# Retention and two feed-forward layers on one core: layer-1 work among the head pairs in units of two f, rectifier on ScalarE

## The chip, the cores and the metric

The kernel runs on one core of one Trainium2 chip. The metric is the device time of one execution in microseconds (us); the number that counts is the median over timed executions. A core has five engines with instruction streams of their own: TensorE (PE in the profile, with its weight loads as PEld), VectorE (DVE), ScalarE (ACT), GpSimd (POOL), and SyncE (SP), which issues the DMAs. They meet only at semaphores. Each engine takes its own instructions in the order of the program.

## What is computed

```
scores = scale * q @ k.T                 # 4 batches, 8 heads, 576 positions, head size 64
ret    = scores * gamma ** rel           # causal: 0 where the key lies after the query
x      = ret @ v                         # -> 2304 tokens x 512
h1 = x @ w1_in    (512 x 2048);  x = max(0.01 * h1, h1) @ w1_out   (2048 x 512)
h2 = x @ w2_in    (512 x 2048);  out = (h2 - tanh(h2)) @ w2_out    (2048 x 512)
```

The weights come in as 64-bit floats. Everything else is 32 bits wide.

## The kernel before

**Weights.** Each layer has 16 blocks f of 128 hidden columns, and each f two weight pieces, one in and one out, of 128 x 512. A piece is loaded (512 KB), turned from 64 into 32 bits by five operations (`narrow_ops`: begin, clamp, shift, top, low; during the retention begin is on ScalarE and the other four on VectorE, later all five are on VectorE), and split into a rounded high part (ScalarE, L161) and the rest (GpSimd, L162). Activations are split the same way, so a product of two 128-blocks takes three matmuls: high times high, high times low, low times high.

**Layers.** The f are handled in groups of four. A step is one f of one token block: `h_mm` (12 matmuls into h), the nonlinearity (`act_a`, `chain`), and two steps later `o_mm` (12 matmuls, which add up over the four f of a group), then `evac`. Token blocks are 512 wide, and one of 256 in each group. While a group runs, `plan` spreads the narrowing of the next group's eight pieces over its steps.

**Retention.** It runs ahead of the layers over 16 head pairs (4 batches with 4 pairs each). In pair i the program emits `scores(i)` and `scores_tail(i)` (TensorE), `mask(i)` (VectorE, reads both), then the outputs of the pair before: `outputs_far(i-1)`, `outputs_near(i-1)`, then `states_mm(i)`, `finish(i-1)` (xh by ScalarE, xl by VectorE) and `states(i)` (VectorE). A head has four full chunks of 128 positions and a tail of 64. The tail's scores `t_sc` and the tail's output `o_tail` are two ranges of one PSUM tile, `x_a`.

**What lies among the pairs.** Group 0 of layer 1 is begun during the retention: three token blocks of 256 (`EARLY`), 12 steps in all, one f at a time, from pair 5 on (`pace`). Its eight weight pieces are prepared by `fill`, which emits the list `ops` (54 entries, about seven for each piece) between the parts of the pairs; the table `at_pair` says how many entries are done by the end of each pair:

```
            at_pair = [7, 10, 14, 17, 24, 28, 38, 46, 53]
            pace = [0] * (NP + 1) + [1] * 10 + [2]
```

The order of the instructions on each engine is the order in which the program emits them; no scheduler moves them.

Of the kernel before, what the change touches and what calls it, by code (L numbers as in the profile page):

```python
# [18 lines left out]
P = 128  # L19
CH = 128  # L20
# [13 lines left out]
def retention_moe_moe(  # L34
# [152 lines left out]
    def act_a(s):  # L187
# [22 lines left out]
    def chain(s):  # L210
        m, g, t0, n, f = steps[s]
        h = hp.pop(s)[:, :n]
        if m == 0:
            v = tmp.pop(s)[:, :n]
# [8 lines left out]
        gt = pools["g"].tile([P, 2, pools["w"]], F32R, tag="g", name="g")  # L223
        nc.scalar.activation(out=gt[:, 0, :n], in_=v, func=AF.Copy)  # L224
        nc.gpsimd.tensor_tensor(  # L225
# [79 lines left out]
    def retention():  # L305
        with ExitStack() as ac:
            ak = ac.enter_context(tc.tile_pool(name="ak", bufs=1))
            ap_ = ac.enter_context(tc.tile_pool(name="ap", bufs=3))
            pools["t"] = ac.enter_context(tc.tile_pool(name="t0", bufs=2))
            pools["g"] = ac.enter_context(tc.tile_pool(name="g0", bufs=3))  # L310
            cw_pool[0] = ac.enter_context(tc.tile_pool(name="c0", bufs=2))
            ps_s = ac.enter_context(tc.tile_pool(name="ps_s", bufs=1, space=PSUM))
            pools["a"] = ac.enter_context(tc.tile_pool(name="ps_a0", bufs=2, space=PSUM))
            pools["w"] = QW
# [5 lines left out]
            pools["h"] = lambda s: x_b[:, :QW]  # L320

# [5 lines left out]
            bds = [ak.tile([P, 2, TAIL], F32, name=f"bd{i}") for i in range(2)]  # L327
            qk, kv, pts, cs_ = {}, {}, {}, {}
            order = [(b, p) for b in range(B) for p in range(NP)]
# [56 lines left out]
            def scores_tail(i):  # L386
                nc.tensor.matmul(
                    out=t_sc, lhsT=qk[i][:, 0, S - CH:], rhs=bds[i % 2], start=True, stop=True
                )

            def mask(i, sc):
# [10 lines left out]
                for h in range(2):  # L402
                    nc.vector.scalar_tensor_tensor(
                        out=pt[:, h, MAIN:], in0=t_sc[:, h, :], scalar=back[h],
                        in1=cm_sb[:, 0, CH:], op0=ALU.mult, op1=ALU.mult,
                    )
                pts[i] = pt

            def states_mm(i):
                t = kv[i]  # L410
                c_ = ps_s.tile([P, NFULL, 64], F32, tag="c", name="c")
                for c in range(NFULL):
                    for h in range(2):
# [4 lines left out]
                        )  # L418
                cs_[i] = c_

            def states(i):
                b, p = order[i]
                c_, st = cs_.pop(i), sts[i % 2]
                for h in range(2):
# [27 lines left out]

            def outputs_near(i, o_):
                pt, t = pts.pop(i), kv.pop(i)
                for c in range(NCH):
                    dst, cs = chunk_out(o_, c)
# [21 lines left out]
            done, s, pending = [0], 0, False  # L478

            def fill(i, part):  # L480
                a, b = ([0] + at_pair + [len(ops)] * len(order))[i:i + 2]
                now = a + (b - a) * (part + 1) // 3
                for op in ops[done[0]:now]:
                    op()
                done[0] = max(done[0], now)

            t = ap_.tile([P, 2, S], F32, tag="qk", name="qk")
# [20 lines left out]
            for i in range(len(order)):  # L508
                if i + 2 < len(order):
                    load(i + 2)  # L510
                n_steps = pace[i]
                if pending:
                    chain(s - 1)
                pending = n_steps == 2
                if i + 1 < len(order):
# [4 lines left out]
                if i + 1 < len(order):  # L520
                    prep_tail(i + 1)
                if n_steps:
                    h_mm(s)
                    act_a(s)
                fill(i, 0)
                if i:
                    ot = outputs_far(i - 1)
                if n_steps:
                    chain(s)
                    fill(i, 1)  # L530
                if s >= LAG:
                    o_mm(s - LAG)
                if i:
                    outputs_near(i - 1, ot)
                states_mm(i)
                if s >= LAG:
                    evac(s - LAG)
                if i:
                    finish(i - 1, ot)
                fill(i, 1)  # L540
                states(i)
                fill(i, 2)
                s += n_steps
                if n_steps == 2:
                    h_mm(s - 1)
                    act_a(s - 1)
                    o_mm(s - 1 - LAG)
                    evac(s - 1 - LAG)
            assert s == n_early and done[0] >= len(ops)
            last = len(order) - 1  # L550
            chain(s - 1)
            ot = outputs_far(last)
            o_mm(s - 2)
            outputs_near(last, ot)
            finish(last, ot)
            evac(s - 2)
            o_mm(s - 1)
            evac(s - 1)


    def layers():
        with ExitStack() as mc:
# [14 lines left out]
            for q, nxt in zip(groups, groups[1:]):  # L577
# [112 lines left out]
```

## Time and profile before

| | |
|---|---|
| median of 3 timed executions | 929.96 us (928.1 to 932.1) |
| the profiled execution: its time | 927.96 us |
| its span, first to last instruction | 926.1 us |
| TensorE busy | 886.5 us (96%) |
| TensorE's weight loads busy | 739.7 us (80%) |
| VectorE, ScalarE, GpSimd busy | 597.6, 388.0, 468.5 us |
| mean granted TensorE clock | 0.992 of 2.4 GHz |

The profiled execution lies 2.0 us below the median, and its span 1.86 us below its own time. Matmuls overlap, so how long one takes is read from the start of one to the start of the next, not from its length.

### The profile page before, as it was taken

To read this page: it belongs to the slowest core of one execution; us is meant where nothing else is said; L and a number is where in the kernel's file an instruction comes from. 1 tells how busy PE (TensorE), PEld (TensorE's weight loads), DVE (VectorE), ACT (ScalarE), POOL (GpSimd) and SP (SyncE) were. 2 spreads that over 40 slices of the span, in tenths; PEclk is the share of its full clock that TensorE was granted. 3 is DMA by queue.
4 is the path that set the end of the run, shared out by engine and by line. 5 is a ranking of instruction groups with operands and counts; after the bars stand their busy time and mean duration, and the time that the engine had idled before them with its cause. 6 is when DMAs were issued, how large, how long until landed. Compare 5 with 4: busy or idle time off the path is not lost.

```text
span 926.1 us, 12850 instructions
## 1 busy us (share of the span) xinstructions
PE 886.5 (96%) x4832; PEld 739.7 (80%) x4832; DVE 597.6 (65%) x988; ACT 388.0 (42%) x777; POOL 468.5 (51%) x364
## 2 busy tenths in 40 slices
PE   5777999999999999999999999999999999999998
PEld 5677888888888888888888787888888877888886
DVE  5887656656573655546762677758785877755544
ACT  2343332233222322233334555675456455575554
POOL 3544422245223523354646855586557645595444
PEclk9989999999999999999999999999999999999999
DMA  7654421211110011101110011101110011001111
GB/s 276 212 174 150 155 99 47 91 46 46 46 63 30 24 46 69 45 1 46 46 69 24 23 46 69 47 0 46 47 69 24 23 46 69 1 1 46 45 46 69
DMA packets 21662, 58.36 MB, mean 63 GB/s; under 512 B 2528, under 2 KB 2912, under 8 KB 21600
## 3 DMA queue, kind: packets, MB, share of 16 engines
q1 hardware_dynamic: 21024, 57.16, 17.9%
q8 instruction: 38, 0.62, 0.3%
q10 hardware_dynamic: 576, 0.38, 0.1%
q14 instruction: 24, 0.20, 0.1%
HBM read 52.81 MB, written 4.72 MB: 62 GB/s over the span
## 4 chain that ended last, share of the span: by engine, by line
PE 60%; DVE 17%; POOL 11%; issue 6%; ACT 5%; DMA 1%; DVEq 0%; POOLq 0%; ACTq 0%
PE a L251 29%; PE h L181 28%; POOL v L203 5%; POOL g L225 4%; DVE v L219 4%; DVE v L222 3%; ACT g L224 2%; DVE acc L276 2%; DVE st L430 2%; DVE pt L396 2%; PE o L459 2%; POOL wp L162 1%; DVE cw L139 1%; ACT xh L468 1%; DVE cw L134 1%
## 5 line engine op out<-in xcount | busy, mean ns | idle before, releaser
L181 PE MATMUL h<-xh,wp 128*128 128x512 f32 (+1 forms) x1216 | 377.0, 375 | 0.0
L181 PEld LDWEIGHTS h<-xh,wp 128*128 128x128 f32 x1216 | 223.2, 188 | 45.2
L181 PE MATMUL h<-xl,wp 128*128 128x512 f32 (+1 forms) x608 | 228.3, 375 | 0.0
L251 PE MATMUL a<-wp,g 128*128 128x512 f32 x864 | 213.4, 393 | 5.2 <-POOL g L225 5.0
L251 PE MATMUL a<-g,wp 128*128 128x512 f32 (+1 forms) x1008 | 216.3, 364 | 1.9 <-POOL g L225 1.9
L225 POOL TENSOR_TENSOR g<-a,g 128x512 fp32r<-128x512 f32 (+1 forms) x84 | 107.7, 1283 | 197.8 <-ACT g L224 197.8
L251 PEld LDWEIGHTS a<-g,wp 128*128 128x128 f32 x1008 | 173.6, 192 | 32.3 <-POOL g L225 2.1
L251 PEld LDWEIGHTS a<-wp,g 128*128 128x128 f32 x864 | 160.9, 188 | 43.8 <-POOL g L225 9.2
L225 POOL TENSOR_TENSOR g<-v,g 128x512 fp32r<-128x512 f32 (+1 forms) x80 | 104.0, 1299 | 142.2 <-ACT g L224 142.2
L181 PEld LDWEIGHTS h<-xl,wp 128*128 128x128 f32 x608 | 114.7, 189 | 22.2
L162 POOL TENSOR_TENSOR wp<-cw,wp 128x512 fp32r<-128x512 f32 x64 | 90.4, 1421 | 55.1 <-ACT wp L161 54.6
L145 DVE SCALAR_TENSOR_TENSOR cw<-st,cw 128x512 uint32<-128x512 uint32 x128 | 116.1, 907 | 3.0
L224 ACT ACTIVATE g<-v 128x512 fp32r<-128x512 f32 (+1 forms) x80 | 47.2, 590 | 163.6 <-DVE v L222 162.5
L193 ACT ACTIVATE a<-h 128x512 f32<-128x512 f32 (+1 forms) x72 | 40.4, 562 | 172.0 <-PE h L181 172.0
L215 DVE TENSOR_TENSOR a<-h,a 128x512 f32<-128x512 f32 (+1 forms) x72 | 46.3, 643 | 101.0 <-ACT a L193 101.0
L203 POOL TENSOR_TENSOR v<-t,u 128x512 f32<-128x512 f32 (+1 forms) x80 | 101.9, 1273 | 11.9 <-ACT t L202 11.8
L276 DVE TENSOR_TENSOR acc<-a,acc 128x512 f32<-128x512 f32 (+1 forms) x114 | 72.0, 659 | 51.9 <-PE a L251 51.8
L219 DVE SCALAR_TENSOR_TENSOR v<-q,v 128x512 f32<-128x512 f32 (+1 forms) x80 | 58.3, 728 | 59.0 <-POOL v L203 58.0
L218 DVE TENSOR_TENSOR h<-h,t 128x512 f32<-128x512 f32 (+1 forms) x80 | 51.2, 640 | 48.4 <-ACT t L202 48.4
L224 ACT ACTIVATE g<-a 128x512 fp32r<-128x512 f32 (+1 forms) x84 | 47.9, 570 | 80.7 <-DVE a L215 80.7
L139 DVE TENSOR_SCALAR cw<-cw 128x512 uint32<-128x512 uint32 x64 | 63.4, 991 | 1.5
L222 DVE COPY_PREDICATED v<-mk,h 128x512 f32<-128x512 uint32 (+1 forms) x80 | 55.1, 688 | 8.2
(56 smaller groups left out, 745.9 us busy)
## 6 DMA issues: line engine op xcount, KB each, us to landing
st<-in_w1i SPq DMA_DIRECT2D x16, 512.0 KB, 3.3
st<-in_w1o SPq DMA_DIRECT2D x16, 512.0 KB, 3.3
st<-in_w2i SPq DMA_DIRECT2D x16, 512.0 KB, 3.2
st<-in_w2o SPq DMA_DIRECT2D x16, 512.0 KB, 3.2
kv<-in_vn SPq DMA_DIRECT2D x16, 320.0 KB, 4.3
qk<-in_qT SPq DMA_DIRECT2D x16, 288.0 KB, 2.9
qk<-in_kT SPq DMA_DIRECT2D x16, 288.0 KB, 3.4
out<-acc SPq DMA_DIRECT2D x18, 256.0 KB, 2.1
```

The costliest lines, as they stand in the source:

```text
L139: nc.vector.tensor_scalar(out=t["w"], in0=t["w"], scalar1=3, scalar2=0x3FFFFFF8, op0=ALU.logical_shift_left, op1=ALU.bitwise_and,)
L145: nc.vector.scalar_tensor_tensor(out=t["w"], in0=t[src], scalar=scalar, in1=t["w"], op0=op, op1=ALU.bitwise_or)
L162: nc.gpsimd.tensor_tensor(out=wp[:, 1, :], in0=wf, in1=wp[:, 0, :].bitcast(F32), op=ALU.subtract)
L181: nc.tensor.matmul(out=ps[:, :n], lhsT=w[:, wi, cs], rhs=x[:, kk, t0:t0 + n], start=kk == 0 and i == 0, stop=kk == KK - 1 and i == 2,)
L203: nc.gpsimd.tensor_tensor(out=v[:, :n], in0=t_[:, :n], in1=u[:, :n], op=ALU.mult)
L218: nc.vector.tensor_tensor(out=h, in0=h, in1=t_, op=ALU.subtract)
L219: nc.vector.scalar_tensor_tensor(out=v, in0=q, scalar=RHO_A, in1=v, op0=ALU.add, op1=ALU.mult)
L222: nc.vector.copy_predicated(out=v, mask=mk.bitcast(U32), data=h)
L224: nc.scalar.activation(out=gt[:, 0, :n], in_=v, func=AF.Copy)
L225: nc.gpsimd.tensor_tensor(out=gt[:, 1, :n], in0=v, in1=gt[:, 0, :n].bitcast(F32), op=ALU.subtract)
L251: nc.tensor.matmul(out=o, lhsT=l, rhs=r, start=f == 0 and i == 0 and d % pack == 0, stop=f == GF - 1 and i == 2 and (d + 1) % pack == 0, s ...
L276: nc.vector.tensor_tensor(out=dst, in0=a, in1=dst, op=ALU.add)
```

## The change

During the retention, group 0 of layer 1 now takes six blocks of 256 tokens instead of three. They run in units of two f (24 matmuls into one bank `x_b`, 24 out of it), one unit a pair from pair 5 on and one behind the last pair: 12 units for 24 steps. In a pair the unit stands ahead of the outputs of the pair before. The tail's output moves from `x_a` to a tile `x_c` that it shares with the chunk states. The pieces are prepared by the end of pair 6. In both layer-1 paths the rectifier is two ScalarE operations that each read PSUM (`Prelu`), one for the full value and one for its rounded part; the maximum on VectorE is gone. In the layers, group 0 keeps one block of 256 and one of 512 tokens instead of three of 512.

```diff
-    QW, EARLY = 256, 3
+    QW, EARLY = 256, 6
...
-                blocks += [(t, min(512, NT - t)) for t in range(EARLY * QW, NT, 512)]
+                blocks += rest + [b for b in big if b[0] >= EARLY * QW]
...
             a = tp.tile([P, W], F32, tag="u", name="a")
-            nc.scalar.activation(out=a[:, :n], in_=h, func=AF.Copy, scale=0.01)
-            tmp[s] = a
+            gt = pools["g"].tile([P, 2, W], F32R, tag="g", name="g")
+            nc.scalar.activation(out=a[:, :n], in_=h, func=AF.Prelu, alpha=0.01)
+            nc.scalar.activation(out=gt[:, 0, :n], in_=h, func=AF.Prelu, alpha=0.01)
+            tmp[s] = a, gt
...
-            nc.vector.tensor_tensor(out=v, in0=h, in1=v, op=ALU.max)
...
-            x_a = ps_s.tile([P, 512], F32, name="x_a")
-            x_b = ps_s.tile([P, 512], F32, name="x_b")
-            t_sc = x_a[:, :2 * TAIL].rearrange("p (h r) -> p h r", h=2)
-            o_tail = x_a[:, QW:QW + TAIL]
+            x_a = ps_s.tile([P, 2, TAIL], F32, name="x_a")
+            x_b = ps_s.tile([P, 2, QW], F32, name="x_b")
+            x_c = ps_s.tile([P, 512], F32, name="x_c")
+            c_ = x_c[:, :NFULL * 64].rearrange("p (c d) -> p c d", d=64)
+            o_tail = x_c[:, NFULL * 64:NFULL * 64 + TAIL]
...
-                for src, lo, hi in ((ot, 0, MAIN), (o_tail, MAIN, S)):
+                for src, lo, hi in ((o_tail, MAIN, S), (ot, 0, MAIN)):
...
-            at_pair = [7, 10, 14, 17, 24, 28, 38, 46, 53]
-            pace = [0] * (NP + 1) + [1] * 10 + [2]
+            at_pair = [3, 8, 14, 21, 30, 44, 54]
+            first = NP + 1
...
+            def place(u):
+                return u // 2 * QW, u % 2 * 2
+
+            def unit_h(u):
+                t0, f0 = place(u)
+                for f in range(2):
+                    w = wt[0, 0, f0 + f]
+                    for kk in range(KK):
+                        cs = slice(kk * P, (kk + 1) * P)
+                        for j, (wi, x) in enumerate(((0, xh), (0, xl), (1, xh))):
+                            nc.tensor.matmul(
+                                out=x_b[:, f, :], lhsT=w[:, wi, cs], rhs=x[:, kk, t0:t0 + QW],
...
+                nc.scalar.activation(out=a, in_=x_b, func=AF.Prelu, alpha=0.01)
+                nc.scalar.activation(out=gt[:, 0], in_=x_b, func=AF.Prelu, alpha=0.01)
+                nc.gpsimd.tensor_tensor(
+                    out=gt[:, 1], in0=a, in1=gt[:, 0].bitcast(F32), op=ALU.subtract
+                )
...
+            def unit_evac(u):
+                t0, f0 = place(u)
+                if f0 == 0:
+                    return
+                ps = accs.pop(u // 2)
+                dst = acc_t[:, :, t0:t0 + QW]
+                nc.scalar.activation(out=dst[:, 2:], in_=ps[:, 2:], func=AF.Copy)
+                nc.vector.tensor_copy(out=dst[:, :2], in_=ps[:, :2])
+
+            def pair_steps(i, fast):
+
+                nonlocal u
+                if fast:
+                    unit_h(u)
+                    fill(i, 1)
+                    if u:
+                        unit_o(u - 1)
+                        unit_evac(u - 1)
+                    u += 1
+                if i:
+                    ot = outputs_far(i - 1)
+                    outputs_near(i - 1, ot, [NFULL])
+                    outputs_near(i - 1, ot, range(NFULL))
+                    del pts[i - 1], kv[i - 1]
+                if i < len(order):
+                    states_mm(i)
+                if i:
+                    finish(i - 1, ot)
+                if i < len(order):
+                    states(i)
...
-                free = max(last + 1, lo + 11)
+                free = max(last + 1, lo + 9)
```

`unit_o(u)` emits the 24 matmuls that take the two f of a unit into the sums of its block; `fill(i, 0)` stands ahead of `pair_steps` and `fill(i, 2)` behind it.

TensorE's instructions of one pair in the middle of the retention, from the last matmul into h on, before (names: x_b is h, a the sums of layer 1, o and x_a the pair's outputs, c the states, sc the scores; a row's last figure is how many instructions it stands for):

```order
L181 MATMUL x_b<-xh,wp 128x256
L447 MATMUL o<-qk,st_96 128x128 x3
L447 MATMUL x_a<-qk,st_96 128x64
L251 MATMUL a<-g,wp 128x256 x12
L459 MATMUL o<-pt,kv 64x128 x8
L459 MATMUL x_a<-pt,kv 64x64 x2
L415 MATMUL c<-kv 64x64 x8
L381 MATMUL sc<-qk 128x128 x8
L387 MATMUL x_a<-bd_98,qk 128x128
```

and the same place now:

```order
L499 MATMUL x_b<-xh,wp 128x256
L524 MATMUL a<-g,wp 128x256 x24
L446 MATMUL o<-qk,st_97 128x128 x3
L446 MATMUL x_c<-qk,st_97 128x64
L458 MATMUL x_c<-pt,kv 64x64 x2
L458 MATMUL o<-pt,kv 64x128 x8
L415 MATMUL x_c<-kv 64x64 x8
L382 MATMUL sc<-qk 128x128 x8
```

The layer's matmuls now stand in one piece ahead of the pair's outputs, and the tail's output no longer goes to the tile that the tail's scores are read from.

VectorE's instructions of pair 6, from its masks to the last one ahead of the next pair's masks, before (pt is the masked scores, cw a weight piece being narrowed, L215 the maximum of the rectifier):

```order
L396 SCALAR_TENSOR_TENSOR pt<-sc,cm_sb 128x512 x2
L403 SCALAR_TENSOR_TENSOR pt<-x_a,cm_sb 128x64 x2
L366 TENSOR_TENSOR qk<-qk,qt_sb 128x64
L134 TENSOR_SCALAR cw<-cw 128x512
L139 TENSOR_SCALAR cw<-cw 128x512
L215 TENSOR_TENSOR a<-x_b,a 128x256
L145 SCALAR_TENSOR_TENSOR cw<-st,cw 128x512 x2
L469 TENSOR_TENSOR xl<-o,xh 128x512
L469 TENSOR_TENSOR xl<-x_a,xh 128x64
L430 SCALAR_TENSOR_TENSOR st_96<-st_96,c 64x64 x6
L134 TENSOR_SCALAR cw<-cw 128x512
L139 TENSOR_SCALAR cw<-cw 128x512
```

and now:

```order
L397 SCALAR_TENSOR_TENSOR pt<-sc,cm_sb 128x512 x2
L404 SCALAR_TENSOR_TENSOR pt<-x_a,cm_sb 128x64 x2
L367 TENSOR_TENSOR qk<-qk,qt_sb 128x64
L145 SCALAR_TENSOR_TENSOR cw<-st,cw 128x512 x2
L134 TENSOR_SCALAR cw<-cw 128x512
L139 TENSOR_SCALAR cw<-cw 128x512
L468 TENSOR_TENSOR xl<-x_c,xh 128x64
L468 TENSOR_TENSOR xl<-o,xh 128x512
L429 SCALAR_TENSOR_TENSOR st_97<-st_97,x_c 64x64 x6
L145 SCALAR_TENSOR_TENSOR cw<-st,cw 128x512 x2
```

The maximum is gone and six narrowing operations stand in the pair, which is the last that holds any; in pair 5 there are eight now, where there were two.

## Rows read from the trace of the kernel before

**Rows 1.** Stretches: length, busy time of each engine, granted clock, DMA share, GB/s.
```profile
40.12:69.06 28.94, 21.26 (x239) 19.74 (x235) 23.96 (x55) 11.17 (x33) 15.24 (x13) 0.88 0.61 196
114.30:121.70 7.40, 7.10 (x88) 6.58 (x88) 4.14 (x15) 2.39 (x8) 3.12 (x3) 1.00 0.50 161
210.11:926.10 715.99, 705.12 (x3265) 580.83 (x3263) 453.90 (x664) 319.67 (x599) 383.09 (x292) 1.00 0.12 41
```
**Rows 2.** Waits of TensorE, 40.12 to 143.45 us: total, times, longest.
```profile
PE x_a L447 <- DVE pt L403: 13.4, 10, 3.3
```
**Rows 3.** Timeline of TensorE, pair 14, then two rows of pair 6: start, length.
```profile
120.37 1.16 PE L381 MATMUL sc<-qk 64*128 64x128 f32 x16
...
121.71 0.36 PE L181 MATMUL x_b<-xh,wp 128*128 128x256 f32 x1
...
123.21 0.83 PE L447 MATMUL o<-qk,st 128*128 128x128 f32 x6
124.34 0.43 PE L447 MATMUL x_a<-qk,st 128*128 128x64 f32 x2 [0.29 <-DVE pt L403]
124.58 1.67 PE L251 MATMUL a<-g,wp 128*128 128x256 f32 x12
126.19 1.09 PE L459 MATMUL o<-pt,kv 128*64 128x128 f32 x16
...
127.79 1.16 PE L381 MATMUL sc<-qk 64*128 64x128 f32 x16
...
53.08 0.83 PE L447 MATMUL o<-qk,st 128*128 128x128 f32 x6
53.74 0.33 PE L447 MATMUL x_a<-qk,st 128*128 128x64 f32 x2
```
**Rows 4.** Timeline of TensorE: starts of pairs 5 and 8, a late stretch of pair 8.
```profile
40.12 1.16 PE L381 MATMUL sc<-qk 64*128 64x128 f32 x16
...
69.06 1.16 PE L381 MATMUL sc<-qk 64*128 64x128 f32 x16
...
75.67 2.91 PE L251 MATMUL a<-g,wp 128*128 128x256 f32 x12
```
**Rows 5.** Timeline of TensorE: the layers' first matmul; a step of 256 tokens.
```profile
143.45 0.49 PE L181 MATMUL h<-xh,wp 128*128 128x512 f32 x1
...
457.49 0.28 PE L181 MATMUL h<-xh,wp 128*128 128x256 f32 x1
...
460.33 0.28 PE L181 MATMUL h<-xh,wp 128*128 128x256 f32 x1
```
**Rows 6.** The chain that ended last: a step of 512 tokens.
```profile
154.82 2.80 PE h L181 x12
157.63 2.75 PE a L251 x12
```
**Rows 7.** Groups of VectorE, 7 to 91.4 us: busy, mean ns of one, idle before.
```profile
L145 DVE SCALAR_TENSOR_TENSOR cw<-st,cw 128x512 uint32<-128x512 uint32 x16 | 16.5, 1028 | 0.3
...
L139 DVE TENSOR_SCALAR cw<-cw 128x512 uint32<-128x512 uint32 x8 | 5.9, 743 | 0.2
L134 DVE TENSOR_SCALAR cw<-cw 128x512 f32<-128x512 f32 x8 | 4.8, 603 | 3.0 <-ACT cw L124 3.0
...
L215 DVE TENSOR_TENSOR a<-x_b,a 128x256 f32<-128x256 f32 x5 | 2.1, 423 | 2.0 <-ACT a L193 2.0
```
**Rows 8.** Timeline of VectorE: masks of pair 5; two shifts of a weight piece.
```profile
45.15 1.29 DVE L396 SCALAR_TENSOR_TENSOR pt<-sc,cm_sb 128x512 f32<-128x512 f32 x2
...
153.17 1.49 DVE L139 TENSOR_SCALAR cw<-cw 128x512 uint32<-128x512 uint32 x1
...
164.96 0.43 DVE L139 TENSOR_SCALAR cw<-cw 128x512 uint32<-128x512 uint32 x1
```
**Rows 9.** Timeline of GpSimd, around the first of these shifts.
```profile
153.08 1.29 POOL L225 TENSOR_TENSOR g<-a,g 128x512 fp32r<-128x512 f32 x1 [3.08 <-ACT g L224]
```
**Rows 10.** Groups by shape: the rectifier's ScalarE operation on 512 columns.
```profile
L193 ACT ACTIVATE a<-h 128x512 f32<-128x512 f32 x60 | 35.9, 598 | 156.2 <-PE h L181 156.2
```

More of the change, by code (lines that the diff above doesn't have):

```diff
@@ L222, in chain @@
             nc.vector.copy_predicated(out=v, mask=mk.bitcast(U32), data=h)
-        gt = pools["g"].tile([P, 2, pools["w"]], F32R, tag="g", name="g")
-        nc.scalar.activation(out=gt[:, 0, :n], in_=v, func=AF.Copy)
+            gt = pools["g"].tile([P, 2, pools["w"]], F32R, tag="g", name="g")
+            nc.scalar.activation(out=gt[:, 0, :n], in_=v, func=AF.Copy)
         nc.gpsimd.tensor_tensor(
@@ L387, in scores_tail @@
                 nc.tensor.matmul(
-                    out=t_sc, lhsT=qk[i][:, 0, S - CH:], rhs=bds[i % 2], start=True, stop=True
+                    out=x_a, lhsT=qk[i][:, 0, S - CH:], rhs=bds[i % 2], start=True, stop=True
                 )
@@ L403, in mask @@
                     nc.vector.scalar_tensor_tensor(
-                        out=pt[:, h, MAIN:], in0=t_sc[:, h, :], scalar=back[h],
+                        out=pt[:, h, MAIN:], in0=x_a[:, h, :], scalar=back[h],
                         in1=cm_sb[:, 0, CH:], op0=ALU.mult, op1=ALU.mult,
@@ L451, in outputs_far, with outputs_near @@
                 return o_
-            def outputs_near(i, o_):
-                pt, t = pts.pop(i), kv.pop(i)
-                for c in range(NCH):
+            def outputs_near(i, o_, chunks):
+                pt, t = pts[i], kv[i]
+                for c in chunks:
                     dst, cs = chunk_out(o_, c)
@@ L475, in retention @@
             ops = piece_ops(pieces)
[L476 to L478 removed]
+            at_pair = [3, 8, 14, 21, 30, 44, 54]
+            first = NP + 1
+            done, u = [0], 0
             def fill(i, part):
@@ L485, in fill @@
                 done[0] = max(done[0], now)
+            gs, accs = {}, {}
+            def place(u):
[9 more added lines that the diff above has]
+                                out=x_b[:, f, :], lhsT=w[:, wi, cs], rhs=x[:, kk, t0:t0 + QW],
+                                start=f == 0 and kk == 0 and j == 0,
+                                stop=f == 1 and kk == KK - 1 and j == 2, skip_group_check=True,
+                            )
+                a = t0_.tile([P, 2, QW], F32, tag="u", name="a")
+                gt = g0_.tile([P, 2, 2, QW], F32R, tag="g", name="g")
+                nc.scalar.activation(out=a, in_=x_b, func=AF.Prelu, alpha=0.01)
+                nc.scalar.activation(out=gt[:, 0], in_=x_b, func=AF.Prelu, alpha=0.01)
+                nc.gpsimd.tensor_tensor(
+                    out=gt[:, 1], in0=a, in1=gt[:, 0].bitcast(F32), op=ALU.subtract
+                )
+                gs[u] = gt
@@ new lines, in unit_o @@
+            def unit_o(u):
+                t0, f0 = place(u)
+                gt = gs.pop(u)
+                if f0 == 0:
+                    accs[u // 2] = ps_a.tile([P, KK, QW], F32, tag="a", name="a")
+                ps = accs[u // 2]
+                for f in range(2):
+                    w = wt[0, 1, f0 + f]
+                    for d in range(KK):
+                        for j, (wi, gi) in enumerate(((0, 0), (0, 1), (1, 0))):
+                            nc.tensor.matmul(
+                                out=ps[:, d, :], lhsT=w[:, wi, d * P:(d + 1) * P],
+                                rhs=gt[:, gi, f, :],
+                                start=f0 + f == 0 and j == 0 and d % 2 == 0,
+                                stop=f0 + f == GF - 1 and j == 2 and d % 2 == 1,
+                                skip_group_check=True,
+                            )
@@ new lines, in unit_evac @@
+            def unit_evac(u):
+                t0, f0 = place(u)
+                if f0 == 0:
+                    return
[23 more added lines that the diff above has]
+                    states(i)
@@ L510, in retention @@
                     load(i + 2)
[L511 to L514, printed above, removed]
+                fast = i >= first
                 if i + 1 < len(order):
@@ L521, in retention @@
                     prep_tail(i + 1)
-                if n_steps:
-                    h_mm(s)
-                    act_a(s)
                 fill(i, 0)
[L526 to L541, printed above, removed]
-                fill(i, 2)
[L543 to L558, printed above, removed]
+                pair_steps(i, fast)
+                fill(i, 2)
+            pair_steps(len(order), True)
+            assert done[0] >= len(ops)
+            unit_o(u - 1)
+            unit_evac(u - 1)
+            assert 2 * u == n_early
     def layers():
```

17 lines of the change are left out of this document (7 added, 10 removed).

## The prediction

> **What bounds the kernel now.** I first cut the span into stretches [rows 1]. From 210.11 us to the end TensorE is busy 705.12 of 715.99 us at full clock: there the layers are bound by their matmuls, and nothing that only moves work can gain. The first stretch is different: from pair 5 (40.12) to pair 8 (69.06) TensorE is busy 21.26 of 28.94 us and its granted clock is 0.88, so part of that time ran at the lower of its two levels. VectorE is busy 23.96 us there. The waits say who ends last [rows 2]: between pair 5 and the layers TensorE waits 13.4 us, ten times, at the output of the tail, for VectorE's masks. That output lies in the tile from which the mask reads the tail's scores, so the outputs of pair i-1 stand behind the mask of pair i, and the masks stand behind the narrowing of the weights.
>
> In pair 14 nothing is narrowed, and the same wait is left in small [rows 3]. From scores to scores it takes 127.79 - 120.37 = 7.42 us. The matmuls into h take 123.21 - 121.71 = 1.50, those out of it 126.19 - 124.58 = 1.61. Between the first far output and the tail lie 124.34 - 123.21 = 1.13, where pair 6, without a wait, needs 53.74 - 53.08 = 0.66. So a pair alone is 7.42 - 1.50 - 1.61 - 0.47 = 3.84 us of TensorE at full clock.
>
> **The layers, what is taken out.** Twelve steps of 512 tokens become four of 512 and four of 256. A step of 512 is 2.80 + 2.75 = 5.55 us [rows 6], one of 256 is 460.33 - 457.49 = 2.84, or 0.118 a matmul [rows 5]. That is 8 x 5.55 - 4 x 2.84 = 33.0 us less. The price is that group 0 is down to 4 x 5.55 + 4 x 2.84 = 33.6 us in which the next eight pieces must be narrowed. By [rows 7] a piece needs 0.603 + 0.743 + 2 x 1.028 = 3.40 us on VectorE, and its first operation, also on VectorE here, is of the clamp's kind, some 0.6: 4.0, or 32 us for eight. That fits only just, but VectorE is no longer on the way from h to g: the maximum has gone, and the rounded part comes from ScalarE directly. So late narrowing delays no activation, only weights, of which the first four are wanted at the end of the 33.6 us and the rest up to two steps later. I cost it at nothing; if that cover is gone it is the few us by which the 32 grow.
>
> **The retention, what is put in.** The added 288 matmuls of 0.118 are 34 us, so the change gains only what TensorE now loses. A pair with a unit is 3.84 + (1.50 + 1.61) + 24 x 0.118 = 9.78 us; I use 9.8. Does anything else need longer? VectorE works 4.14 us in pair 14 [rows 1], maximum included; ScalarE 2.39, to which the longer rectifier adds under 1; GpSimd one subtraction of 128x512, 1.29 [rows 9], in place of a narrower one. The unit stands ahead of the outputs and gives 5.9 us in which the states of the pair before get done, and the tail's output no longer waits for a mask. So from the pair on in which the weights are complete, TensorE is alone on the path, without the 0.47.
>
> Prelu is not in this trace. Below it is bounded by nothing, above by the two operations whose place it takes; the nearest row is the scaled copy from PSUM, 0.598 us [rows 10], which I take. Two of them, 1.2 us, lie under the 24 other matmuls of the unit before (2.8 us) and far from ScalarE's limit, so even twice the length moves nothing.
>
> **A rule against it.** The Trainium skill (ScalarE: Activation LUTs, Rules for kernel authors) says that relu and max belong on VectorE and not on ScalarE. The rows here speak for the other choice: TensorE waits for VectorE, and two maxima of 0.423 [rows 7] in pairs 5, 6 and 7 would be some 2.5 us more on it. By that rule the sum below would be worse by up to that and not better; no run here shows Prelu yet.
>
> **Pairs 5 to 7, where weights are late.** All eight pieces are now wanted by pair 7. I walk VectorE. The masks of pair 5 began at 45.15 [rows 8]. Four more narrowing operations stand ahead of them now (2 x 1.028 + 0.603 + 0.743 = 3.4 us [rows 7]), but VectorE's waits behind the masked tail go; between 45.2 and 48.6 I take 46.2, since those waits were spread over four pairs. Pair 5 is 4.14 less the maximum, 3.8, and eight operations, 4 x 1.028 + 2 x (0.603 + 0.743) = 6.8: masks of pair 6 at 56.8, say 57, because a clamp must await its ScalarE operation. Piece 5, which the second half of unit 0 needs, is split by ScalarE behind an operation that awaits these masks and the tail's preparation: 57 + about 1.9, about 0.5 for that operation, 0.6 for the copy [rows 10] and 1.3 for GpSimd [rows 9] is 61.3. TensorE by then has done all else and waits some 5 us. Then 12 x 0.118 = 1.4, the outputs and states of pair 5 (3.84 less scores and their tail, 121.71 - 120.37 = 1.34 [rows 3]) 2.5, scores 1.3, and h of unit 2, 2.9: 69.4, the first half of unit 1's outputs to 70.8. Piece 7 is narrowed last, behind finish and states of pair 6: outputs done 65.2, ScalarE 0.8, VectorE 2.4 and two joins 2.06, then 0.6 and 1.3: 72.4. The other 12 matmuls and the outputs follow, 1.4 + 2.5: pair 8 begins at 76.3. One stretch like [rows 4], where 12 matmuls took 2.91 instead of 1.67 us behind a wait, and another of part of it, make it 78.0, against 69.06.
>
> **The sum.** From 78.0, eight pairs of 9.8 are 78.4. Behind the last pair come 24 matmuls into h and 24 out (5.9), the last outputs (2.5 less 0.6 for states, 1.9) and 24 more out (2.9): 10.7. The last rectifier and subtraction lie under the 4.9 us of matmuls between. The layers begin at 167.1 instead of 143.45 [rows 5]: 23.65 later, and they are 33.0 shorter, which is -9.35. The profiled execution's 927.96 becomes 918.6; it stands 2.0 below the median of the runs, so as a median I expect **920.6 us**.
>
> **Rivals.** *The weights do not hold.* If VectorE gets through pairs 5 and 6 with its short forms (a shift took 0.43 at 164.96 [rows 8]), TensorE alone sets them: 40.12 + (3.84 + 2.92) + 2 x 9.8 = 66.5, which is 11.5 earlier: 909.1.
>
> *The narrowing is slower than its mean.* The shift at 153.17 took 1.49 us beside a GpSimd subtraction of 153.08 to 154.37, that at 164.96 only 0.43 [rows 8, 9]. Pairs 5 and 6 pack 14 narrowing operations beside more GpSimd work than before. At 1.49 each instead of a mean of 0.88 ((6.8 + 5.5) / 14) that is 8.6 us: 929.2, no change. The Trainium skill (Advanced Engine Details and Errata, VectorE Performance Modes) says that VectorE's second SBUF port is shared with GpSimd, and that two-port VectorE operations and GpSimd block each other; the trace agrees, 1.49 against 0.43.
>
> *The steady wait only moves.* The tail's output now shares x_c with the states, which VectorE reads late in a pair. If that costs the 0.47 us that the mask cost, in eight pairs, 3.8: 924.4. Against it: 5.9 us of matmuls stand between that read and the next tail.
>
> *The clock, and slower.* The waits of some 5 us in pair 6 and of 1 to 3 in pair 7 are longer than the longest of 3.3 before [rows 2], and the clock was 0.88 among those [rows 1]. Twelve matmuls lose 1.24 us at the lower level [rows 4]. If pairs 6 and 7 ran at it throughout, their 2 x 9.8 us would take as long again, and this beyond what I added: some 18 us, 938.6. It decides from 9.35 us on, about half of the two pairs. Against it: back-to-back units of 5.9 us are the longest unbroken matmul stretches that the retention has had, and in the steady pairs the clock is 1.00 [rows 1].
>
> **Chances.** Forecast (915.5 to 925.3, the unknowns of the walk, mostly the anchor of 45.2 to 48.6 and one us or two in the two pairs) 0.62; weights do not hold 0.13; slow narrowing 0.14; steady wait 0.06; clock 0.05. The range that leaves out no more than 2 in 10 goes from 909 to 927: it cuts off the full price of slow narrowing, the clock, and the very end of the first rival. A measurement of this kernel tells about 0.5%, 4.6 us, from no change, so faster is below 925.3. Nearly all of the forecast, the first rival and most of the third lie there: 0.80. The same, 925.3 to 934.6, is slow narrowing and what is left: 0.15. Slower is the clock: 0.05.
>
> **What would show it.** The layers' first matmul near 167 (161 to 172 for the forecast), with the pairs from 8 on at 9.7 to 10.0 us from scores to scores and no wait of TensorE in them. In pair 6 one wait of TensorE at the matmuls out of h, for GpSimd's weight split, of 3 to 6 us, and a smaller one in pair 7. The wait for the masks at the tail's output gone. A group 0 in the layers with TensorE unbroken, and behind it the trace of before, shifted. ScalarE's Prelu at 0.55 to 0.7 us on 512 columns. I am wrong if steady pairs take more than 10.3, if pair 8 begins ahead of 72 or behind 82, if group 0 has waits above 2 us, or if the time after 210 us of the old trace does not simply shift.

## The result, and the profile after

| | before | after |
|---|---|---|
| median of timed executions | 929.03 us (927.44 to 932.10, 4 of them) | 916.56 us (915.52 to 918.17, 4 of them) |
| profiled execution, span | 927.96 us, 926.1 us | 915.52 us, 913.7 us |
| TensorE busy, mean clock | 886.5 us, 0.992 | 881.9 us, 0.992 |
| VectorE busy | 597.6 us | 537.5 us |

The ratio is 0.9858 with an interval of 0.9839 to 0.9877: 1.4% faster, some 13 us of 929, with 12.4 us between the two profiled executions. The prediction was 920.6 us, from 909 to 927.

The stretches of the kernel after (length, busy time of TensorE, its weight loads, VectorE, ScalarE and GpSimd, granted clock, DMA share, GB/s): pairs 6 and 7, the eight pairs from pair 8 on but for their last 0.56 us (the last unit begins at 154.64), and the layers up to group 1.

```profile
46.42:77.74 31.32, 22.99 (x224) 21.33 (x221) 18.99 (x41) 12.30 (x29) 15.77 (x12) 0.89 0.35 114
77.74:154.08 76.34, 76.34 (x868) 74.36 (x866) 33.18 (x107) 22.89 (x66) 28.06 (x22) 1.00 0.37 122
165.41:193.46 28.05, 28.05 (x171) 24.93 (x169) 25.95 (x38) 10.55 (x23) 10.83 (x10) 1.00 0.32 110
```

They answer to [rows 1]. In the first stretch TensorE still stands still for 8 us, at a clock of 0.89. In the second it is busy 76.34 of 76.34 us, with VectorE at less than half. The third is group 0 of the layers, which is wholly TensorE's, while VectorE is busy 25.95 of 28.05 us.

TensorE's waits from the start to 175 us, in total, times and longest:

```profile
PE a L524 <- ACT wp L161: 5.7, 1, 5.7
PE sc L382 <- POOL qk L354: 5.6, 1, 5.6
PE o L446 <- DVE st L429: 2.7, 3, 1.7
PE sc L382 <- POOL kv L359: 1.9, 1, 1.9
...
PE x_b L499 <- POOL wp L162: 0.9, 1, 0.9
```

The ten waits for the masks [rows 2] are gone. In their place stands one of 5.7 us for the split of a weight piece, in pair 6. The wait for `qk` was there before (5.5 us): it is the start of the kernel.

TensorE's timeline (start, length, instructions, the wait in brackets), in pair 6, pair 8, and at the layers' first matmul:

```profile
60.11 0.79 PE L524 MATMUL a<-g,wp 128*128 128x256 f32 x2 [5.70 <-ACT wp L161]
61.46 2.50 PE L524 MATMUL a<-g,wp 128*128 128x256 f32 x10 [0.56 <-POOL wp L162]
63.76 1.48 PE L446 MATMUL o<-qk,st 128*128 128x128 f32 x6
...
67.37 1.16 PE L382 MATMUL sc<-qk 64*128 64x128 f32 x16
...
73.91 1.46 PE L524 MATMUL a<-g,wp 128*128 128x256 f32 x10 [0.47 <-POOL wp L162]
...
77.74 1.16 PE L382 MATMUL sc<-qk 64*128 64x128 f32 x16
78.83 0.49 PE L388 MATMUL x_a<-bd,qk 128*128 128x128 f32 x2
79.08 0.36 PE L499 MATMUL x_b<-xh,wp 128*128 128x256 f32 x1
...
82.00 2.98 PE L524 MATMUL a<-g,wp 128*128 128x256 f32 x24
84.81 0.83 PE L446 MATMUL o<-qk,st 128*128 128x128 f32 x6
85.48 0.33 PE L446 MATMUL x_c<-qk,st 128*128 128x64 f32 x2
...
87.35 1.16 PE L382 MATMUL sc<-qk 64*128 64x128 f32 x16
...
165.41 0.28 PE L181 MATMUL h<-xh,wp 128*128 128x256 f32 x1
```

A pair with its unit takes 87.35 - 77.74 = 9.61 us, without a wait, against 7.42 for a pair with one step before [rows 3]. The layers begin at 165.41, against 143.45 [rows 5]: 22.0 us later. From there to the end it is 913.7 - 165.41 = 748.3 us, against 926.1 - 143.45 = 782.65: 34.4 less.

Behind the wait of 5.70 us the ten matmuls of 61.46 take 2.3 us to the next start, where 24 took 2.81 in pair 8. The clock (the last figure but two) in the second half of that pair, from 56.75 on, and in the next pair:

```profile
56.75:67.37 10.62, 6.70 (x57) 6.23 (x57) 4.57 (x10) 2.90 (x6) 2.52 (x2) 0.68 0.21 67
67.37:77.74 10.37, 9.89 (x114) 9.43 (x111) 6.37 (x16) 4.38 (x11) 6.27 (x5) 1.00 0.33 107
```

A mean of 0.68 is a stretch spent in good part at the lower level; in pair 7, whose longest wait is 0.47 us, the clock is whole again. The released weight piece on ScalarE:

```profile
58.88 0.52 ACT L371 ACTIVATE bd<-qk 64x64 f32<-64x64 f32 x2 [4.08 <-DVE qk L367]
59.43 0.63 ACT L161 ACTIVATE wp<-cw 128x512 fp32r<-128x512 f32 x1
```

VectorE at that time:

```profile
57.17 1.29 DVE L397 SCALAR_TENSOR_TENSOR pt<-sc,cm_sb 128x512 f32<-128x512 f32 x2
...
58.63 0.22 DVE L367 TENSOR_TENSOR qk<-qk,qt_sb 128x64 f32<-128x64 f32 x1
```

ScalarE idles 4.08 us in front of its part of the next tail, for VectorE's part at 58.63, which stands behind the masks of pair 6 (57.17); the split stands behind that in ScalarE's program. So the wait that the profile books on `wp` is a wait for the masks of pair 6, one queue further on.

### The profile page after: what moved, and what is told of

It is laid out like the page before. It is cut to its first block, busy times and chain, and to the rows that moved or that the text cites. A ratio compares the mean times of both kernels' runs of the same rounds, so it can differ in the third digit from the quotient of the medians.

```text
span 913.7 us, 13160 instructions
## 1 busy us (share of the span) xinstructions
PE 881.9 (97%) x5024; PEld 745.6 (82%) x5024; DVE 537.5 (59%) x902; ACT 377.0 (41%) x767; POOL 462.2 (51%) x360
## 5 line engine op out<-in xcount | busy, mean ns | idle before, releaser
L181 PE MATMUL h<-xh,wp 128*128 128x512 f32 (+1 forms) x1184 | 360.8, 371 | 0.0
L181 PEld LDWEIGHTS h<-xh,wp 128*128 128x128 f32 x1184 | 215.7, 188 | 42.2
L181 PE MATMUL h<-xl,wp 128*128 128x512 f32 (+1 forms) x592 | 219.6, 371 | 0.0
L253 PE MATMUL a<-g,wp 128*128 128x512 f32 (+1 forms) x816 | 176.8, 365 | 2.1 <-POOL g L227 2.1
L253 PEld LDWEIGHTS a<-g,wp 128*128 128x128 f32 x816 | 141.4, 188 | 28.7 <-POOL g L227 2.3
L227 POOL TENSOR_TENSOR g<-a,g 128x512 fp32r<-128x512 f32 (+1 forms) x68 | 84.7, 1248 | 130.7 <-ACT g L195 113.3
L181 PEld LDWEIGHTS h<-xl,wp 128*128 128x128 f32 x592 | 111.3, 188 | 20.8
L205 POOL TENSOR_TENSOR v<-t,u 128x512 f32<-128x512 f32 (+1 forms) x80 | 102.1, 1276 | 11.2 <-ACT t L204 11.1
L206 ACT ACTIVATE q<-u,qb 128x512 f32<-128x512 f32 (+1 forms) x80 | 54.4, 680 | 0.0
L209 ACT ACTIVATE mk<-u,qb 128x512 f32<-128x512 f32 (+1 forms) x80 | 54.2, 677 | 0.0
L139 DVE TENSOR_SCALAR cw<-cw 128x512 uint32<-128x512 uint32 x64 | 49.1, 767 | 1.7
```

Of the source, the lines that this page charges most:

```text
L139: nc.vector.tensor_scalar(out=t["w"], in0=t["w"], scalar1=3, scalar2=0x3FFFFFF8, op0=ALU.logical_shift_left, op1=ALU.bitwise_and,)
L181: nc.tensor.matmul(out=ps[:, :n], lhsT=w[:, wi, cs], rhs=x[:, kk, t0:t0 + n], start=kk == 0 and i == 0, stop=kk == KK - 1 and i == 2,)
L205: nc.gpsimd.tensor_tensor(out=v[:, :n], in0=t_[:, :n], in1=u[:, :n], op=ALU.mult)
L206: nc.scalar.activation(out=q[:, :n], in_=u[:, :n], func=AF.Square, scale=math.sqrt(RHO_C), bias=qb[:, 0:1])
L227: nc.gpsimd.tensor_tensor(out=gt[:, 1, :n], in0=v, in1=gt[:, 0, :n].bitcast(F32), op=ALU.subtract)
L253: nc.tensor.matmul(out=o, lhsT=l, rhs=r, start=f == 0 and i == 0 and d % pack == 0, stop=f == GF - 1 and i == 2 and (d + 1) % pack == 0, s ...
```

## The experiments

The change has two halves: (a) the tail's output moved to the tile of the states, and the rectifier moved to ScalarE; (b) six blocks in units of two f, one a pair, ahead of the outputs. The theory was the prediction's: (b) fills TensorE's waits, (a) brings little alone. Ratios are to the kernel before on the same chip.

**The tail alone**, in the kernel before:

```diff
-            o_tail = x_a[:, QW:QW + TAIL]
+            x_c = ps_s.tile([P, 512], F32, name="x_c")
+            c_ = x_c[:, :NFULL * 64].rearrange("p (c d) -> p c d", d=64)
+            o_tail = x_c[:, NFULL * 64:NFULL * 64 + TAIL]
...
-                c_ = ps_s.tile([P, NFULL, 64], F32, tag="c", name="c")
```

> The kernel before with one part of the change: the tail's output shares a tile with the states instead of with the tail's scores. Theory (the gain is TensorE's waits in pairs 5 to 15, which the units fill because they stand ahead of the outputs): the tail no longer waits for the mask, but the next scores still need the scores' bank, which the same mask reads, so in pairs 5 to 8 the wait goes there; the steady pairs lose their 0.47 us each. -2 to -5 us, 924 to 927. Rival (the gain comes from the tail's output leaving the tile): -9 to -13 us, 916 to 920, and no wait of TensorE for masks at all.

Measured: 919.21 us, ratio 0.9886 (0.9872 to 0.9901), some 10 us faster. The theory missed, the rival was right. TensorE's waits from 35 us on in this kernel, and two neighbouring steady pairs:

```profile
PE o L447 <- ACT st L426: 4.5, 5, 1.7
PE sc L383 <- POOL kv L360: 3.1, 3, 1.7
```
```profile
107.55 1.16 PE L383 MATMUL sc<-qk 64*128 64x128 f32 x16
...
114.53 1.16 PE L383 MATMUL sc<-qk 64*128 64x128 f32 x16
...
137.17 0.49 PE L181 MATMUL h<-xh,wp 128*128 128x512 f32 x1
```

No wait for a mask is left. What takes their place is 7.6 us in these eight waits (and one of 0.3 us for a maximum), against 13.4 in ten [rows 2], and a steady pair takes 6.98 instead of 7.42 [rows 3]: its 0.47 us have gone. The layers begin 6.3 us earlier in the profiled execution, whose span is 7.6 us shorter (its time, 920.25, is the longest of this kernel's).

**The rectifier alone**, in the kernel before, as in the change's diff (`act_a` and `chain` only):

> The kernel before with one part of the change: the rectifier as two ScalarE operations from PSUM, no maximum on VectorE, in both layer-1 paths. Theory: VectorE is relieved of 0.42 us in each of the pairs 5 to 9, where it ends last, and of nothing that matters in the layers: -1 to -3 us, 926 to 928. Rival (the relief of VectorE is most of the gain): -8 us or more, below 921.

Measured: 927.37 us, ratio 0.9982 (0.9963 to 1.0002): some 2 us, as the theory has it, with an interval that just reaches no change. The masks still hold TensorE up (`x_a`, 14.4 us from 35 us on, 15.0 before).

**The rectifier taken back**, in the kernel after: the scaled copy by ScalarE, the maximum by VectorE, the rounding copy by ScalarE, in the units (the maximum behind the fill that follows a unit's h) and in the layers.

```diff
-                nc.scalar.activation(out=a, in_=x_b, func=AF.Prelu, alpha=0.01)
-                nc.scalar.activation(out=gt[:, 0], in_=x_b, func=AF.Prelu, alpha=0.01)
+                nc.vector.tensor_tensor(out=a, in0=x_b, in1=a, op=ALU.max)
+                nc.scalar.activation(out=gt[:, 0], in_=a, func=AF.Copy)
```

> The changed kernel with the rectifier as before: a scaled copy by ScalarE, the maximum on VectorE, the rounded copy by ScalarE, in the units and in the layers. Theory (the rectifier's place is worth what VectorE gains in pairs 5 to 7 and nothing elsewhere): the maximum over both f is 0.7 us on VectorE in each of pairs 5 and 6, and the layers' group 0 with its steps of 256 stays without waits: +1 to +3 us against the changed kernel's 916.6. Rival (the layers' group 0, half as long now, can hold its narrowing only without the maximum): waits of TensorE between 165 and 200 us, and +4 us or more.

Measured: 917.04 us, ratio 0.9862 (0.9836 to 0.9887). Against the change's 0.9858 this is no difference clear of noise: less than the theory's 1 to 3 us. The rival, waits in group 0, did not come. The wait of pair 6 has only another name (`x_b` for VectorE's maximum, 5.1 us).

**The unit behind the outputs**, in the kernel after: in `pair_steps` the block that emits the outputs of the pair before is moved ahead of `if fast:`.

> The changed kernel, the unit behind the outputs of the pair before instead of ahead of them; nothing else. Theory: the unit no longer covers the states of the pair before (a ScalarE copy and six VectorE operations, some 2.3 us behind the states' matmuls, against 1.35 us of scores), so each steady pair waits 1 us or a little more at the far outputs: +8 to +14 us against the changed kernel, 924 to 931, and a wait for VectorE's states in every pair. Rival (that the pairs hold two f at once is what counts, not where they stand): within 2 us of the changed kernel's 916.6.

Measured: 930.41 us, ratio 1.0008 (0.9996 to 1.0019): the whole gain is gone, as the theory has it. TensorE, pair 8 to 9:

```profile
78.26 1.16 PE L382 MATMUL sc<-qk 64*128 64x128 f32 x16
79.35 0.49 PE L388 MATMUL x_a<-bd,qk 128*128 128x128 f32 x2
79.96 1.27 PE L446 MATMUL o<-qk,st 128*128 128x128 f32 x6
81.24 0.43 PE L446 MATMUL x_c<-qk,st 128*128 128x64 f32 x2
...
89.21 1.16 PE L382 MATMUL sc<-qk 64*128 64x128 f32 x16
```

and VectorE at the far outputs:

```profile
79.73 1.46 DVE L429 SCALAR_TENSOR_TENSOR st<-st,x_c 64x64 f32<-64x64 f32 x6
```

A pair takes 10.95 us, with the same matmuls as the 9.61. The far outputs follow on the scores at once: the first begins 0.61 us behind the scores' tail (79.96 - 79.35), where in the change the next matmul follows on it by 0.25 (79.08 - 78.83), and six of them take 1.28 us instead of the 0.67 of 84.81 to 85.48 above. Both together are 0.97 of the 1.34 us that the pair is longer. In that time VectorE writes the six states that these matmuls read (79.73 to 81.19), so I read the stretch as matmuls that are let go one by one. The list of waits does not show it in the steady pairs: it has 7.6 us for VectorE's states from 35 us on, in three waits, none of them in pairs 8 to 15, where the change has no such wait. 1.34 us in each of eight pairs are 10.7 of the 13.9 us.

**Four blocks**, in the kernel after: `EARLY = 4`, the last two blocks of 256 back in the layers as one of 512, so pair 13 has only the matmuls out of the last unit, and pairs 14 and 15 have nothing.

> The changed kernel with four early blocks instead of six: 8 units in pairs 5 to 12, none in pairs 13 to 15 and behind them, and one more block of 512 in the layers' group 0. Theory: a unit costs as much among the pairs as it saves in the layers (5.7 to 5.8 us for 5.55 in a step of 512), so only the three pairs without a unit lose, in which TensorE has 3.84 us of work while VectorE, ScalarE and their handshakes need 5.5 to 6.3 as in pairs 2 to 4: +4 to +8 us against the changed kernel, 920 to 925. Rival (each block moved brings its share of the 12.5 us): a third of the gain is lost, +4.2, with the steady pairs without a unit at 4 us, not above 5. Second rival (the number of blocks does not matter): within 1.5 us of 916.6.

Measured: 926.27 us (920.95 to 928.28, ratio 0.9956, 0.9928 to 0.9983), profiled at 922.64: 7.1 us slower than the change between profiled executions, 9.7 by the medians, where 4 to 8 was expected. TensorE, the last two pairs:

```profile
132.72 1.16 PE L382 MATMUL sc<-qk 64*128 64x128 f32 x16
...
137.67 1.16 PE L382 MATMUL sc<-qk 64*128 64x128 f32 x16
...
144.54 1.27 PE L446 MATMUL o<-qk,st 128*128 128x128 f32 x6 [1.63 <-DVE st L429]
...
148.82 0.39 PE L181 MATMUL h<-xh,wp 128*128 128x256 f32 x1 [1.42 <-DVE xl L468]
```

A pair without a unit takes 137.67 - 132.72 = 4.95 us where its matmuls need 3.84, and two more waits, 1.63 and 1.42 us, follow ahead of the layers. So a unit in a pair covers about 1.1 us. The pair's 4.95 us are less than the 5.5 to 6.3 that the theory gave it, and just under the 5 of its first rival, whose price of 4.2 us the time exceeds. With a like loss in pair 15 the pairs and the two waits make 5 to 6 of the 7.1 us; another 1.5 lie at the change of layers, where this kernel's clock falls and the change's does not (last section). The spread of the runs, 7 us, is wider than that of any other kernel here: the three slowest have a mean clock of 0.983, the fastest 0.992. What sets it stays open.

**The tail taken back**, in the kernel after: `x_a` a whole tile again that holds `t_sc` and `o_tail`.

> The changed kernel with the tail's output back in the tile of the tail's scores, so that it waits for the mask of the pair again. Moving the tail alone has given 10 us to the kernel before. Theory A (the units stand ahead of the outputs and cover the masks, so that from pair 8 on the tail's place is worth nothing, and only pairs 1 to 7 lose): +2 to +5 us, 918.5 to 921.5, steady pairs still 9.6 us. Theory B (the tail's place is what the change is worth, in the changed kernel as in the old one): +8 to +12 us, 925 to 929, with waits for the masks also in the steady pairs.

Measured: 919.30 us, ratio 0.9888 (0.9862 to 0.9914): 2.7 us slower, as Theory A has it. The steady pairs keep their 9.61 us; the waits of `x_a` from 35 us on are two, one of 3.8 us for the masks and one of 4.3 us of the next scores' tail for `xl`, which VectorE makes from the output in the same tile. So in the new form the move is worth some 3 us by the medians, with intervals that overlap, where in the old form it was worth 10.

**Both of (a), none of (b)**: the kernel before with the tail and the rectifier of the change; three blocks, old order.

> The kernel before with two parts of the change, the tail's output beside the states and the rectifier by ScalarE alone; still three early blocks, one f at a time, inside the outputs. Theory (the parts add up): 919.2 less 1 to 2, that is 917 to 918.5, so that the units, the order and the other three blocks are worth only what is left, 1 to 2 us. Rival (the rectifier and the tail relieve the same wait): 919 or more.

Measured: 915.99 us, ratio 0.9847 (0.982 to 0.9875), a median below both expectations: as fast as the whole change. TensorE's longest waits from 35 us on, a steady pair, and the layers' first matmul:

```profile
PE sc L385 <- POOL kv L362: 3.1, 3, 1.6
PE o L449 <- ACT st L428: 3.0, 4, 1.5
```
```profile
103.13 1.16 PE L385 MATMUL sc<-qk 64*128 64x128 f32 x16
...
110.11 1.16 PE L385 MATMUL sc<-qk 64*128 64x128 f32 x16
...
132.31 0.48 PE L181 MATMUL h<-xh,wp 128*128 128x512 f32 x1
```

The layers begin 11.1 us earlier than before, more than the 6.3 of the tail and the 1.85 of the rectifier alone (it began them at 141.6) give together. That the two do more than add is not shown by the times: the product of the single ratios, 0.9886 x 0.9982 = 0.9868, lies inside the interval. Part of the surplus is the clock: from 35 us to the layers it is 1.00 here, 0.98 with the tail alone, 0.96 with the rectifier alone and 0.95 before.

**None of (a), all of (b)**: the change with the tail and the rectifier both taken back (the edits of the two runs above).

> The changed kernel with both parts undone that alone make the old form as fast as the new one: the tail's output back beside the tail's scores and the maximum back on VectorE; what is left are the units of two f, their place ahead of the outputs, and six blocks. Theory (substitutes: either the tail and the rectifier take the wait away, or the units cover it; one alone brings nearly all): 919 to 922, steady pairs 9.6 us, and the waits for the masks only up to pair 7. Rival (the parts add, and the units bring nothing by themselves): 926 to 930.

Measured: 921.09 us, ratio 0.9915 (0.9885 to 0.9945), as the theory has it. From 35 us on `x_a` makes TensorE wait three times, 8.2 us in all, twice of that for masks (3.7). The four corners:

| | (a) as before | (a) as in the change |
|---|---|---|
| old form, three blocks | 1 (929.03) | 0.9847 (915.99) |
| units, six blocks | 0.9915 (921.09) | 0.9858 (916.56) |

If the halves added, the last corner were 0.9847 x 0.9915 = 0.976, or 907 us. It lies where (a) alone lies. The two halves are in the main substitutes: (a) takes away the stop for the masks, (b) covers it from pair 7 on and leaves the 8.2 us, and what one has taken the other can't take again. But (b) also brings a wait of its own, the 5.70 us of pair 6, and the next run shows what that hides.

**The split one entry earlier**, in the kernel after. ScalarE's split of piece 5 is one entry of `ops`, and `at_pair` put it behind the wait for the masks:

```diff
-            at_pair = [3, 8, 14, 21, 30, 44, 54]
+            at_pair = [3, 8, 14, 21, 30, 45, 54]
```

> The changed kernel with one number changed, 44 to 45 in the table of pair 5: the split of piece 5, for which TensorE waits 5.7 us in pair 6, is emitted at the end of pair 5 and no longer behind the masks of pair 6. Theory (that wait is on the path, and it is long because ScalarE's copy stands behind the masks): the copy runs at about 56 instead of 59.4, the wait falls to 2 to 3 us, -2.5 to -4.5 us, 912 to 914. Rival (VectorE's narrowing sets the time anyway): the wait comes back in pair 7, within 1 us of 916.6.

Measured: 911.91 us, ratio 0.9803 (0.9775 to 0.9831). One execution, the profiled one, took 3648 us and is left out of this. Its trace says nothing of the edit (TensorE is busy for 3637.1 of 3646.6 us, a matmul of 512 columns 1216 ns long on average against 396 in the change, at a granted clock of 1.000), and the same kernel ran again:

> The same kernel as the run before it with 45 for 44 in the table of pair 5, once more for its trace, which was lost to one execution of 3.6 ms. Its median was 911.9. Theory: 911 to 913, ScalarE's copy of piece 5 at about 56 to 57 us and TensorE's wait for it 2 to 3 us instead of 5.7. Rival: the wait is found again in pair 7.

Measured: 911.13 us, ratio 0.9805 (0.9776 to 0.9834): by one number of a table 5.4 us less than the change by the medians, 3.5 between the profiled executions; the intervals of the ratios don't overlap. ScalarE and TensorE of this kernel:

```profile
56.64 0.61 ACT L161 ACTIVATE wp<-cw 128x512 fp32r<-128x512 f32 x1
```
```profile
58.38 3.26 PE L524 MATMUL a<-g,wp 128*128 128x256 f32 x24
61.48 0.83 PE L446 MATMUL o<-qk,st 128*128 128x128 f32 x6
...
74.30 1.16 PE L382 MATMUL sc<-qk 64*128 64x128 f32 x16
```

The split runs at 56.64 instead of 59.43. The 24 matmuls out of h go in one piece, 61.48 - 58.38 = 3.1 us, the far outputs behind them take 0.83 us instead of the 1.48 of 63.76 in the change, and pair 8 begins 3.4 us earlier, as do the layers (161.97). The longest wait left in pairs 5 to 8 is one of 3.0 us, for the rectifier of the unit before to have read `x_b`: the fill now puts an operation ahead of it on ScalarE.

This bears on the table of the four corners as well. With the entry moved, (b) on top of (a) goes from 0.9847 to 0.9805, some 4 us (intervals 0.982 to 0.9875 and 0.9776 to 0.9834, which overlap a little). So part of what (b) seems not to give is what its own late split takes away.

**Half of unit 0's outputs later as well** (the second f behind the outputs of pair 5):

> The changed kernel with 45 for 44 and, in pair 6 alone, the second half of unit 0's outputs behind the outputs of pair 5. Theory: TensorE does the 2.5 us of pair 5's outputs while it waits for piece 5, as soon as VectorE's states of pair 5 are done, so a further -1 to -2 us against 45 alone: 909.5 to 911.5, with no wait for a weight split above 1 us. Rival (the states of pair 5 come as late as the split): within 0.7 us of 45 alone.

Measured: 911.98 us, ratio 0.9816 (0.9782 to 0.985), 0.1 and 0.9 above the two runs of the kernel with the entry alone: no further gain, as the rival has it. No wait for a weight split above 1 us is left, as the theory has it, and the profiled execution begins the layers 1.07 us earlier (160.90), but the medians don't show it; the wait of 3.0 us for the rectifier stays.

**Light narrowing**, in the kernel after (three of the five operations left out for these eight pieces), timed in one execution:

```diff
+        if early[0]:
+            return [begin, lambda: None, lambda: None, lambda: None, low]
```

> The changed kernel with three of the five narrowing operations (clamp, shift and top, all on VectorE) left out of the eight pieces of the retention, so that its weights are not the reference's. This prices what the narrowing costs TensorE in pairs 0 to 7. Theory: pair 8 begins 8 to 12 us earlier than at 77.7, between 66 and 70, steady pairs 9.6, the whole 904 to 908. Rival (with the narrowing away the pairs are bound by the handshakes between masks, outputs and states): pair 8 at 73 or later, 911 or more.

Measured: 909.28 us, between the theory (904 to 908) and its rival (from 911 on). Pair 8 begins at 70.5, the layers at 158.18, 7.2 us earlier. The longest wait that remains is 3.1 us, still for ScalarE's split of a piece.

## Why the prediction was right, point by point

- **The early pairs.** Pair 8 was forecast at 78.0 and began at 77.74; the masks of pair 6 at 57 began at 57.17, the second half of the weights at 61.3 was used at 61.46, and the wait of some 5 us was 5.70. The anchor was off: pair 5 began at 38.10, not at 40.12, and its masks at 44.61, not 46.2, which was luck: the eight operations took the 6.8 us of the walk, and VectorE then waited 1.96 us for a clamp's ScalarE operation, which the walk had at next to nothing. Of the narrowing, shifts took 0.43 to 1.38 us in these pairs, so the rival of slow narrowing did not come. Nor did the rival that the weights hold nothing. Its price was too high as well: with most of the narrowing left out, pair 8 begins 7.2 us earlier, not 11.5, since VectorE then idles 3.3 us for ScalarE's `xh` ahead of the masks of pair 6.
- **The steady pair** was the term that was mis-sized in the retention: 9.61, not 9.8. The 9.78 took over pair 14's 1.50 + 1.61 us for 24 matmuls, 3.1 us, which hold seams that a unit has once and not twice; 48 take 84.81 - 79.08 = 5.73 us. From pair 8 to the last unit (154.64) it is 76.90 us for 78.4.
- **The end of the retention** was 10.77 for 10.7.
- **The layers** were 33.0 us less by the sum. Up to the first h of group 1 it is 61.13 before (to 204.58) and 28.05 after: 33.1. Group 0 had no wait, though VectorE was at 93%. Behind that the span is another 1.3 us shorter, which no edit accounts for: it is the clock at the change of layers (last section), so luck. With the 1.5 and 0.3 of the pairs that makes the 3.1 us by which the profiled execution's 915.52 lies below the 918.6.
- **The clock rival** came in half a pair, at 0.68 in the second half of pair 6 and not in pair 7: the ten matmuls of 61.46 and the outputs behind them cost 2.3 + 3.6 us where 1.2 + 2.5 were due, 2.2 us, near the 1.7 put in for it, far from the 18 of the rival.
- **The steady wait only moves**: it did not; no wait stands in these pairs.
- **Prelu** on 512 columns takes 599 ns (L506) and 592 ns (L507), against the 598 that the scaled copy gave [rows 10].
- **The rule against it.** In rows: the maximum back on VectorE makes no difference in the new form, and its removal from the old form 1.9 us with the masks in place, 3.2 us with the tail moved (919.21 to 915.99, with intervals of the ratios that just touch). So the move to ScalarE is worth between nothing and 3 us here and costs nothing. The Trainium skill (ScalarE: Activation LUTs, Rules for kernel authors) puts relu and max on VectorE; here, on 32-bit data, that was never the faster choice.
- **Wrong was whose gain it is.** "The change gains only what TensorE now loses" is true of the sum, but the prediction had the units fill those losses and priced the tail's place at the 0.47 us of a steady pair. The tail's place alone is worth 10 us in the old form: the outputs of pair i-1 stand behind the masks of pair i only because of the shared tile. With that gone (915.99) the three further blocks, as the change places their weights, bring nothing by the medians: the retention grows from 132.31 to 165.41, by 33.1 us, and the layers give back 783.2 - 748.3 = 34.9.

## What to carry to other kernels

Before work is moved into a wait, ask what makes the wait: here two unrelated ranges in one PSUM tile, undoing that alone brought 10 of the 13 us, and with the shorter way through the rectifier all of them. Two cures of one wait don't simply add, so each is to be priced with the other in place. And look at the queue of the engine that releases: the costliest wait that was left was one instruction standing behind another engine's masks, and moving it up by one entry of a table was worth 3.5 us between the profiled executions and some 5 by the medians.

## What the runs showed of the hardware

**The clock at like places.** At the change of layers TensorE has a like wait in these kernels, about 2 us for GpSimd's `g`, but not the same clock around it. Stretches of 25 us, in the kernel before and after:

```profile
457.00:482.00 25.00, 23.10 (x128) 20.27 (x127) 19.09 (x28) 8.74 (x18) 16.02 (x14) 0.93 0.17 57
```
```profile
445.88:470.88 25.00, 22.88 (x134) 20.02 (x133) 19.04 (x24) 7.95 (x17) 16.86 (x14) 1.00 0.19 64
```

The same matmuls out of h around the wait, before and after:

```profile
458.91 1.59 PE L251 MATMUL a<-g,wp 128*128 128x256 f32 x12
...
463.93 2.33 PE L251 MATMUL a<-g,wp 128*128 128x256 f32 x11 [1.90 <-POOL g L225]
...
469.66 1.59 PE L251 MATMUL a<-g,wp 128*128 128x256 f32 x12
```
```profile
447.78 1.59 PE L253 MATMUL a<-g,wp 128*128 128x256 f32 x12
...
453.03 1.57 PE L253 MATMUL a<-g,wp 128*128 128x256 f32 x11 [2.12 <-POOL g L227]
...
457.23 1.59 PE L253 MATMUL a<-g,wp 128*128 128x256 f32 x12
```

From the first to the last of these rows it is 10.75 us before and 9.45 after, though the wait is the longer one after: the eleven matmuls behind it take 2.33 us at the lower level and 1.57 at full clock. From 204.58 (before) and 193.46 (after) to the first row, and from the last row to the end of the span, the two kernels agree within 0.03 us. So this place is the whole of the 1.3 us that the sum lacks. The kernel with the tail alone waits 1.90 us here, as the kernel before does, and has 1.00 (451.00 to 476.00); with four blocks the wait is 2.12 us, as in the change, and the clock 0.93 (446.00 to 471.00). Why the clock falls in one kernel and not in the other stays open; runs of one kernel differ by 2 to 5 us in any case.

**What the waits cost besides.** From 35 us to the layers the mean clock is 0.95 before, over 108.45 us. With 1.2 of 2.4 GHz as the lower level, that is some 11 us at that level and up to some 5 us of TensorE's time lost (an estimate from these figures); with both parts of (a) the clock there is 1.00. So a part of what the masks' waits cost is not in the list of waits.

**One slow execution.** In the execution of 3648 us every kind of matmul is slow and the granted clock on record is 1.000. Why stays open.
